# Attention with its eight PSUM banks split four and four and its outputs turned a step later; sums spread at the change of thirds

## The chip, the cores and the metric

One Trainium2 chip, of which the kernel uses one core. TensorE (PE) multiplies into PSUM, which this kernel uses as eight banks of 128 x 512 fp32; VectorE (DVE) and ScalarE (ACT) read PSUM, GpSimd (POOL) works on SBUF in this kernel, and SyncE (SP) issues the DMAs. The metric is the device time of one execution in microseconds.

## The reference, cut to what matters

```python
def phi(x):                                   # attention with random features
    proj = einsum('bhsd,md->bhsm', x, omega)
    h = proj - sum(x * x, -1) / 2
    return exp(h - max(h, -1)) / sqrt(m)
q_p, k_p = phi(q * scale), phi(k * scale)
kv = einsum('bhsm,bhsd->bhmd', k_p, v);  z = sum(k_p, 2)
attn = einsum('bhsm,bhmd->bhsd', q_p, kv) / (einsum('bhsm,bhm->bhs', q_p, z) + 1e-6)
x = attn as 2304 tokens x 512
x = (silu(x @ w_gate) * (x @ w_val)) @ w_out                 # 512 -> 1536 -> 512
P = sinkhorn(exp(x @ w_gate2), 8 rounds)                     # 2304 x 8
out = sum over 8 experts e of P[:, e] * (relu(x @ w1[e]) @ w2[e])   # 512 -> 1024 -> 512
```

Batch 4, 8 heads, 576 positions, head size 64, 128 features. All products are made of fp32r parts: a high part (a rounded copy) and a low part (the rest), three matmuls for each product.

## The kernel before

The whole program is issued by hand in one order (`manual_schedule`), so each engine runs what its instructions are in program order. The stages follow one another: attention, the first feed-forward (`moe1`), the first third of the tokens of the experts' layer (`moe2`), and the other two thirds (`thirds`).

**Attention** runs over 36 chunks of 128 x 512 (k tail, then k and q in turns: odd chunks are k, even ones q, up to a q tail at the end). A software pipeline (lines 651 to 666) does in step s for each entry (name, lag) of `ORDER` (line 63) the piece `name` of chunk s - lag. The pieces: `s0` squares x on GpSimd (three instructions, L478 to L481), `s0r` sums them on VectorE into ssq (L487), `s0n` scales that on GpSimd into nsq (L493); `s2p` makes 16 projections on TensorE into two banks (L515); `s2m` takes row maxima mx on VectorE (L519), `s2b` and `s2c` make hm (L523) and the bias bi (L527); `s2x` does eight exponentials on ScalarE out of the two banks (L534); `s3` transposes a q chunk (L559) or multiplies k with v (L555); `s3a` copies the result on ScalarE (L572, L568); `s4` makes numerators and denominators of a q chunk (L585); `s4d`, `s4r`, `s4n` divide on VectorE (L597, L602, L607); `s5` turns the quotient on TensorE (L617), `s5a` copies the high part on ScalarE (L628), and `s5b` takes the low part on VectorE (L633), both out of the bank that `s5` wrote. `pump` issues one piece of the conversion of the next stage's weights (lines 183 to 216), which spreads over ScalarE, VectorE and GpSimd.

`bank(use)` gives the next bank of the ring of that use; rings with the same banks share one turn. Of the eight banks tr3 takes two, and tr5, pr and nu share a ring of six. From step 37 on (line 652) `DRAIN` holds, and after each step `next(m1)` issues a unit of the next stage: 12 matmuls with 384 columns. x and the squares live in one tile of four parts: three for x, one for the squares.

**Thirds**: each step is a product pair over 14 slots: `quad_product` makes hidden units in seven products (a scheme of Strassen's kind) in three banks, each product a slot; `second_product` multiplies the hidden forms of the step before and adds them to sums. The hidden forms of a half are made by `a1` to `a4`, each put off by a slot by `after` (line 1385), as are the additions of sums and the stores at the change from the second to the last third (lines 1416 to 1430). `make_forms` splits the x forms of the next third, one a slot (lines 874 to 894).

Of the kernel before, what the change touches and what calls it, by code (L numbers as in the profile page):

```python
# [21 lines left out]
B, H, S, D = 4, 8, 576, 64  # L22
# [17 lines left out]
NG2 = 2 * E  # L40
# [10 lines left out]
class Kernel:  # L51
    def __init__(self, tc, x, v, vt, omega, wg, wv, wo, w2g, w1, w2, out):
# [7 lines left out]

    ORDER = [("s3a0", 3), ("s0r", 0), ("s5a", 7), ("s2p", 1), ("s2m0", 1), ("s40", 4), ("s41", 4),
# [3 lines left out]
    RINGS = dict(tr3=(0, 3), tr5=(4, 5, 6, 7, 2, 1), pr=(4, 5, 6, 7, 2, 1), nu=(4, 5, 6,  # L67
                 7, 2, 1), a=(0, 1, 2, 3), b=(4, 5, 6, 7))

    DRAIN = dict(RINGS, tr3=(4, 5), tr5=(4, 5), nu=(6, 7))  # L70


    EARLY = 1
# [325 lines left out]
    def attention(self, m1):  # L399
        tc, nc = self.tc, self.nc  # L400
        if True:
            af, ident = self.af, self.ident
            t0 = af.tile([P, 4, 512], F32, tag="t0", name="at0")
            t1 = af.tile([P, 2, 1024], F32, tag="t1", name="at1")
            t2 = af.tile([P, 4, 512], F32, tag="t2", name="at2")
            t3 = af.tile([P, 4, 512], F32, tag="t3", name="at3")
            t4 = af.tile([P, 5, 8, ZW], F32, tag="t4", name="at4")
# [6 lines left out]
            def turn(name, n):  # L414
                rot[name] = (rot.get(name, -1) + 1) % n
                return rot[name]
# [20 lines left out]
            NCH = len(chunks)  # L437
# [5 lines left out]
            def load(i):  # L443
                side, bp, hp, j = chunks[i]
                c = st[i]
                n = 8 if hp is None else 2 * hp + j
                k = turn("x", 3)
                xt = xts[turn("xt", 4)]
                c["xt"] = xt.rearrange("p (a t) -> p a t", t=P)
                c["x"] = t0[:, k].rearrange("p (a d) -> p a d", d=D)  # L450
                for w, t in ((1, xt), (0, t0[:, k])):
                    nc.sync.dma_start(t, self.x["qk".index(side), w, bp, n])
                c["idx"] = (lambda a, h: 2 * a + h) if hp is None else (lambda a, h: 4 * h + a)
# [15 lines left out]
            def s0(i):  # L469
                c = st[i]  # L470
                sqv = c["x"]
                if i < self.EARLY:
                    c["xx"] = t2[:, i].rearrange("p (a d) -> p a d", d=D)
                    c["ssq"] = sm.tile([P, 8], F32, tag="ssq", name=f"ssq{i}", bufs=4)
                    nc.scalar.activation(c["xx"], sqv, AF.Square)
                    return
                xx = t0[:, 3].rearrange("p (a d) -> p a d", d=D)
                nc.gpsimd.tensor_tensor(xx, sqv, sqv, op=ALU.mult)  # L478
                ssq = sm.tile([P, 8], F32, tag="ssq", name=f"ssq{i}", bufs=4)
                nc.gpsimd.tensor_tensor(xx[:, :, 0:32], xx[:, :, 0:32], xx[:, :, 32:64], op=ALU.add)  # L480
                nc.gpsimd.tensor_tensor(xx[:, :, 0:16], xx[:, :, 0:16], xx[:, :, 16:32], op=ALU.add)  # L481
                c["xx"], c["ssq"] = xx, ssq
# [153 lines left out]
            pump = lambda i: self.attn_pump()  # L636
# [11 lines left out]
            load(0)  # L648
            load(1)
            s0(0)  # L650
            for step in range(NCH + 7):
                if step == NCH + 1:
                    self.rings = self.DRAIN
                if step + 2 < NCH:
                    load(step + 2)
                if step == 0:
                    loadv(0)
                if step + 1 < NCH:
                    loadv(step + 1)
                for fn, n in order:  # L660
                    i = step - n
                    if 0 <= i < NCH:
                        fn(i)
                self.attn_hook(step)
                if step >= NCH + 1:
                    next(m1)

    def attn_hook(self, step):
# [205 lines left out]
    def make_forms(self):  # L874

        nc, v, g = self.nc, self.nc.vector, self.nc.gpsimd
        p0, p1, q0, q1 = self.quarters()
        x = self.spot
        low = None
        yield  # L880
        for n, src, eng in (("b11", x, g), ("t1", p0, v), ("t2", q1, v), ("t3", q0, v), (None, None, None), ("t4", p1, v),
                            ("b21", x, g), ("b22", p0, v), (None, None, None)):
            if low is not None:
                low()
                low = None
            if n == "t2":
                self.fetch_one(x, 0, 2)
            if n == "t3":
                self.fetch_one(p0, 1, 2)
            if n:  # L890
                h, l = [self.xslot(i, *self.XS[n]) for i in range(2)]
                nc.scalar.copy(h, src)
                low = lambda l=l, src=src, h=h, eng=eng: eng.tensor_tensor(l, src, f(h), op=ALU.subtract)
            yield
# [361 lines left out]
    def thirds(self, xs, t3, t4):  # L1256
        nc, af, v = self.nc, self.af, self.nc.vector
# [28 lines left out]
        def after(n, fn):  # L1286
            later.setdefault(now[0] + n, []).append(fn)
# [8 lines left out]
        def quad_product(step, j):  # L1296
            m = step % NG2
            k, i = divmod(j, 7)
            n = USE[i]
            c = live  # L1300
# [5 lines left out]
            g, first = {1: ("x", 1), 5: ("z", 1), 6: ("x", 0), 2: ("y", 1), 7: ("x", 0), 3: ("z", 0), 4: ("x", 0)}[n]  # L1306
            g = c[g]
# [7 lines left out]
            p0, p1 = [pb[m // 2 % 2][:, j * NBK:(j + 1) * NBK] for j in range(2)]  # L1315
            x, z, y = c["x"], c["z"], c["y"]
# [20 lines left out]
            if i == 0:  # L1337
                c["s"] = temp()
                nc.scalar.copy(c["s"], x)
            elif i == 1:  # L1340
                c["p"] = temp()
                nc.scalar.copy(c["p"], z)
            elif i == 2:
                c["u"] = temp()
                nc.scalar.copy(c["u"], x)  # L1345
            elif i == 3:
                v.tensor_tensor(c["s"], y, c["s"], op=ALU.add)
                gate(c["s"], c["s"], p0)
            elif i == 4:
                v.tensor_tensor(c["p"], x, c["p"], op=ALU.add)  # L1350
                gate(c["p"], c["p"], p1)
                hi(1, c["s"])
            elif i == 5:
                v.tensor_tensor(c["u"], z, c["u"], op=ALU.add)
                gate(c["u"], c["u"], p1)
                hi(3, c["p"])
                lo(1, c["s"], nc.gpsimd)
            else:
                r11, r22, r12, r21, t1, t2 = c["s"], c["p"], c["u"], temp(), temp(), temp()
                gate(r21, x, p0)  # L1360
                lo(3, r22, nc.gpsimd)

                def a1():
                    sub(t1, r12, r11)
                    sub(r12, r22, r12)
                    sub(t2, r22, t1)
                    hi(2, r21)
                    hi(5, t1)
                    lo(2, r21)

                def a2():
                    sub(r21, r21, t2)
                    hi(7, r12)
                    hi(6, t2)
                    lo(5, t1)
                    lo(7, r12)

                def a3():
                    hi(4, r21)
                    lo(6, t2)  # L1380

                def a4():
                    lo(4, r21)

                for d, fn in enumerate((a1, a2, a3, a4)):
                    after(d + 1, fn)

        def second_product(step, j):
            t, m = divmod(step, NG2)
# [26 lines left out]
            if m == NG2 - 1:  # L1416
                last = step > m
                sums = {1: [(2, 1)], 5: [(3, 5)], 6: [(1, 6), (3, 1)]}
                sums.setdefault(7 if last else 6, []).extend([(7, 1), (4, 7), (5, 7)])
                for k, (d, c) in enumerate(sums.get(n, ())):  # L1420
                    def add(d=d, c=c, eng=nc.gpsimd if d == 5 else v):
                        eng.tensor_tensor(a[d], a[d], a[c], op=ALU.add)

                    if last:
                        add()
                    else:
                        after(k + 1, add)
                for d in {2: (2,), 7: (5,) if last else (), 6: (3,) if last else (3, 5, 4)}.get(n, ()):
                    c, i = {2: (0, 0), 4: (2, 0), 3: (0, 1), 5: (2, 1)}[d]
                    after(0 if last else {2: 3, 3: 5, 5: 8, 4: 7}[d], lambda c=c, i=i, d=d: self.store_block(t + 1, c, i, a[d]))  # L1430

        sums = xg = iter(())
        for g in range(self.STEPS):
# [107 lines left out]
```

## Time and profile before

| | |
|---|---|
| time, median of 3 runs (lowest to highest) | 2070.68 us (2070.24 to 2072.59) |
| the profiled execution: time | 2070.69 us |
| the profiled execution: span of its instructions | 2068.9 us |
| mean granted clock of TensorE | 0.996 |
| TensorE busy | 2017.9 us (98%) |
| VectorE, ScalarE, GpSimd busy | 1369.6, 806.5, 1044.0 us (66%, 39%, 50%) |

Read it so: TensorE is busy almost throughout, so what it does not do matters most; the 40 slices of the page show it below nine tenths only in the first slices, which are attention. Busy time of TensorE is time in which some matmul is in flight, not its peak rate.

### The profile page before, as it was taken

How to read it: one execution, taken by the hardware profiler on the slowest of the kernel's cores; microseconds unless marked ns; L12 is line 12 of the kernel's file. 1: busy time of each engine (PE TensorE's matmuls, PEld its weight loads, DVE VectorE, ACT ScalarE, POOL GpSimd, SP SyncE). 2: the span in 40 equal slices, each digit the busy share in tenths (PEclk: the TensorE clock that was granted, in tenths of full speed). 3: DMA queues.
4: the chain of work that ended last, by engine and by line, in shares of the span. 5: the costliest groups of instructions: out<-in, count | busy, mean ns of one | idle time of the engine just before them, and what ended most of it. 6: DMA issues, size and time to landing. Idle time of an engine off the chain costs nothing.

```text
span 2068.9 us, 34032 instructions
## 1 busy us (share of the span) xinstructions
PE 2017.9 (98%) x12556; PEld 1948.7 (94%) x12556; DVE 1369.6 (66%) x2283; ACT 806.5 (39%) x1805; POOL 1044.0 (50%) x1054
## 2 busy tenths in 40 slices
PE   6889999999999999999999999999999999999998
PEld 6679999999998899899898999999999999999998
DVE  6877788778657644444445666666678666666666
ACT  6784433333335443343342423233333433332322
POOL 6865666656515454554752443434464534343443
PEclk9999999999999999999999999999999999999999
DMA  7644556546236567677678788888878888888784
GB/s 236 198 145 128 178 164 188 183 149 204 82 113 239 198 236 260 220 270 261 221 267 289 251 264 257 261 261 282 276 248 276 273 260 262 258 265 256 245 271 152
DMA packets 238134, 467.85 MB, mean 226 GB/s; under 512 B 20272, under 2 KB 110096, under 8 KB 233872
## 3 DMA queue, kind: packets, MB, share of 16 engines
q1 hardware_dynamic: 237968, 465.68, 68.3%
q8 instruction: 99, 1.62, 0.3%
q14 instruction: 67, 0.55, 0.1%
HBM read 340.25 MB, written 125.35 MB: 225 GB/s over the span
## 4 chain that ended last, share of the span: by engine, by line
PE 90%; DVE 5%; POOL 3%; issue 1%; ACT 1%; DMA 1%; SPq 0%; DVEq 0%; POOLq 0%; ACTq 0%
PE bank L1064 12%; PE bank L1312 7%; PE bank L1314 7%; PE bank L1313 7%; PE pair L1403 7%; PE pair L1405 7%; PE pair L1404 7%; PE bank L704 5%; PE bank L706 5%; PE bank L705 5%; PE bank L1005 4%; PE bank L1007 4%; PE bank L1006 4%; PE bank L736 2%; PE bank L738 2%; PE bank L737 2%
## 5 line engine op out<-in xcount | busy, mean ns | idle before, releaser
L1415 DVE TENSOR_TENSOR sums<-pair,sums 128x768 f32<-128x768 f32 x209 | 198.6, 951 | 43.6 <-PE pair L1405 43.6
L1312 PE MATMUL bank<-xh,ar 128*128 128x384 f32 x564 | 188.7, 335 | 2.4 <-ACT mt L1345 2.0
L1313 PE MATMUL bank<-xl,ar 128*128 128x384 f32 x564 | 188.4, 334 | 0.0
L1314 PE MATMUL bank<-xh,ar 128*128 128x384 f32 x564 | 188.4, 334 | 0.0
L1080 DVE SCALAR_TENSOR_TENSOR ac<-bank,mt,ac 128x512 f32<-128x512 f32 x84 | 63.1, 751 | 131.3 <-PE bank L1064 131.3
L1403 PE MATMUL pair<-xh,ar 128*128 128x384 f32 x344 | 115.0, 334 | 0.1
L1405 PE MATMUL pair<-xh,ar 128*128 128x384 f32 x344 | 114.9, 334 | 0.0
L1404 PE MATMUL pair<-xl,ar 128*128 128x384 f32 x344 | 114.9, 334 | 0.0
L1312 PEld LDWEIGHTS bank<-xh,ar 128*128 128x128 f32 x564 | 105.8, 188 | 3.4 <-ACT mt L1345 2.7
L1313 PEld LDWEIGHTS bank<-xl,ar 128*128 128x128 f32 x564 | 105.9, 188 | 0.0
L1314 PEld LDWEIGHTS bank<-xh,ar 128*128 128x128 f32 x564 | 105.9, 188 | 0.0
L718 ACT CAST ar<-mt 128x384 fp32r<-128x384 f32 x72 | 37.0, 514 | 169.4 <-DVE mt L715 169.4
L704 PE MATMUL bank<-xh,ar 128*128 128x384 f32 x288 | 96.7, 336 | 0.1
L706 PE MATMUL bank<-xh,ar 128*128 128x384 f32 x288 | 96.2, 334 | 0.0
L706 PE MATMUL bank<-xh,ar1b 128*128 128x384 f32 x288 | 96.2, 334 | 0.0
L705 PE MATMUL bank<-xl,ar 128*128 128x384 f32 x288 | 96.2, 334 | 0.0
L704 PE MATMUL bank<-xh,ar1b 128*128 128x384 f32 x288 | 96.2, 334 | 0.0
L705 PE MATMUL bank<-xl,ar1b 128*128 128x384 f32 x288 | 96.2, 334 | 0.0
L534 ACT ACTIVATE at<-bank,bi 128x128 f32<-128x128 f32 x288 | 78.4, 383 | 36.7 <-DVE bi L527 23.7
L1005 PE MATMUL bank<-xh,ar 128*128 128x384 f32 x264 | 89.1, 338 | 0.9 <-DVE mt L1039 0.6
L1007 PE MATMUL bank<-xh,ar 128*128 128x384 f32 x264 | 88.6, 335 | 0.1
L1006 PE MATMUL bank<-xl,ar 128*128 128x384 f32 x264 | 88.4, 335 | 0.0
(369 smaller groups left out, 6652.4 us busy)
## 6 DMA issues: line engine op xcount, KB each, us to landing
ar<-w2forms SPq DMA_DIRECT2D x144, 512.0 KB, 4.4
ar<-w1forms SPq DMA_DIRECT2D x141, 512.0 KB, 4.8
ar1b<-w1forms SPq DMA_DIRECT2D x62, 512.0 KB, 4.8
ar1b<-w2forms SPq DMA_DIRECT2D x61, 512.0 KB, 4.4
w2forms<-ar SPq DMA_DIRECT2D x224, 128.0 KB, 4.0
w1forms<-ar SPq DMA_DIRECT2D x22, 1280.0 KB, 6.9
sumsraw<-in_w_dram SPq DMA_DIRECT2D x32, 512.0 KB, 4.5
w2forms<-sumsraw SPq DMA_DIRECT2D x128, 128.0 KB, 2.7
```

The lines of the kernel that those rows point to most:

```text
L704: nc.tensor.matmul(t, hi[:, c, fs], self.xh[:, c, cs], start=(c == 0), stop=False)
L705: nc.tensor.matmul(t, hi[:, c, fs], self.xl[:, c, cs], start=False, stop=False)
L706: nc.tensor.matmul(t, lo[:, c, fs], self.xh[:, c, cs], start=False, stop=(c == KC - 1))
L1005: nc.tensor.matmul(g, ah[:, c, :], bh[:, c, :], start=(first and c == 0), stop=False, skip_group_check=not first)
L1064: nc.tensor.matmul(y, a, w[:, fi % 2, ds], start=(first and x == 0 and k == 0 and fi == fis[0]), stop=(last and x == 1 and fi == fis[-1]))
L1312: nc.tensor.matmul(g, w[:, 0, d], bh[:, d, :], start=bool(first and d == 0), stop=False, skip_group_check=not first)
L1313: nc.tensor.matmul(g, w[:, 0, d], bl[:, d, :], start=False, stop=False, skip_group_check=not first)
L1314: nc.tensor.matmul(g, w[:, 1, d], bh[:, d, :], start=False, stop=(d == 1), skip_group_check=not first)
L1403: nc.tensor.matmul(y, w[:, k, 0, ds], h, start=(k == 0), stop=False)
L1404: nc.tensor.matmul(y, w[:, k, 0, ds], l, start=False, stop=False)
L1405: nc.tensor.matmul(y, w[:, k, 1, ds], h, start=False, stop=(k == 1))
L1415: v.tensor_tensor(a[n], pair, a[n], op=ALU.add)
```

## The change

It changes five things. (1) In attention the projections (pr) have banks 4 to 7 for themselves, and tr3, tr5 and nu share a ring of banks 0 to 3; in the drain all three use banks 4 to 7. (2) The outputs are turned with lag 7 instead of 6, their high and low parts are made with lag 8 instead of 7, and the low part s5b comes second in the order, ahead of the maxima; s0r moves behind s2c, and s5 ahead of s3. The loop has one step more, and the first unit of the next stage comes a step later, so that their number stays. (3) x has two parts of its tile, the squares two. (4) In `thirds` the pieces a1 to a4 of the very first half, and of the last half before the change of thirds, are put off by two slots each instead of one; the additions and stores at the change from the second third to the last come later. (5) `make_forms` splits t4 last instead of fifth, with an empty slot more.

```diff
--- before.py
+++ after.py
@@ -60,14 +60,15 @@
 
 
 
-    ORDER = [("s3a0", 3), ("s0r", 0), ("s5a", 7), ("s2p", 1), ("s2m0", 1), ("s40", 4), ("s41", 4),
-             ("s2m1", 1), ("s2b", 1), ("s2c", 1), ("s3a1", 3), ("s0", -1), ("pump", 2), ("s2", 0),
-             ("s30", 2), ("s2x0", 1), ("s31", 2), ("s4d0", 4), ("s0n", 0), ("s5", 6), ("s5b",
-             7), ("s2x1", 1), ("s4d1", 4), ("pump", 3), ("s4r", 4), ("s4n0", 4), ("s4n1", 4)]
-    RINGS = dict(tr3=(0, 3), tr5=(4, 5, 6, 7, 2, 1), pr=(4, 5, 6, 7, 2, 1), nu=(4, 5, 6,
-                 7, 2, 1), a=(0, 1, 2, 3), b=(4, 5, 6, 7))
-
-    DRAIN = dict(RINGS, tr3=(4, 5), tr5=(4, 5), nu=(6, 7))
+    ORDER = [("s3a0", 3), ("s5a", 8), ("s5b", 8), ("s2p", 1), ("s2m0", 1), ("s40", 4), ("s41", 4),
+             ("s2m1", 1), ("s2b", 1), ("s2c", 1), ("s0r", 0), ("s3a1", 3), ("s0", -1), ("pump", 2), ("s2", 0),
+             ("s5", 7), ("s30", 2), ("s2x0", 1), ("s31", 2), ("s4d0", 4), ("s0n", 0),
+             ("s2x1", 1), ("s4d1", 4), ("pump", 3), ("s4r", 4), ("s4n0", 4), ("s4n1", 4)]
+    RINGS = dict(tr3=(0, 3, 2, 1), tr5=(0, 3, 2, 1), pr=(4, 5, 6, 7), nu=(0, 3, 2, 1),
+                 a=(0, 1, 2, 3), b=(4, 5, 6, 7))
+
+    DRAIN = dict(RINGS, tr3=(4, 5, 6, 7), tr5=(4, 5, 6, 7), nu=(4, 5, 6, 7))
+
 
 
     EARLY = 1
@@ -444,7 +445,7 @@
                 side, bp, hp, j = chunks[i]
                 c = st[i]
                 n = 8 if hp is None else 2 * hp + j
-                k = turn("x", 3)
+                k = turn("x", 2)
                 xt = xts[turn("xt", 4)]
                 c["xt"] = xt.rearrange("p (a t) -> p a t", t=P)
                 c["x"] = t0[:, k].rearrange("p (a d) -> p a d", d=D)
@@ -474,7 +475,7 @@
                     c["ssq"] = sm.tile([P, 8], F32, tag="ssq", name=f"ssq{i}", bufs=4)
                     nc.scalar.activation(c["xx"], sqv, AF.Square)
                     return
-                xx = t0[:, 3].rearrange("p (a d) -> p a d", d=D)
+                xx = t0[:, 2 + turn("xx", 2)].rearrange("p (a d) -> p a d", d=D)
                 nc.gpsimd.tensor_tensor(xx, sqv, sqv, op=ALU.mult)
                 ssq = sm.tile([P, 8], F32, tag="ssq", name=f"ssq{i}", bufs=4)
                 nc.gpsimd.tensor_tensor(xx[:, :, 0:32], xx[:, :, 0:32], xx[:, :, 32:64], op=ALU.add)
@@ -648,7 +649,7 @@
             load(0)
             load(1)
             s0(0)
-            for step in range(NCH + 7):
+            for step in range(NCH + 8):
                 if step == NCH + 1:
                     self.rings = self.DRAIN
                 if step + 2 < NCH:
@@ -662,7 +663,7 @@
                     if 0 <= i < NCH:
                         fn(i)
                 self.attn_hook(step)
-                if step >= NCH + 1:
+                if step >= NCH + 2:
                     next(m1)
 
     def attn_hook(self, step):
@@ -878,8 +879,9 @@
         x = self.spot
         low = None
         yield
-        for n, src, eng in (("b11", x, g), ("t1", p0, v), ("t2", q1, v), ("t3", q0, v), (None, None, None), ("t4", p1, v),
-                            ("b21", x, g), ("b22", p0, v), (None, None, None)):
+        wait = (None, None, None)
+        for n, src, eng in (("b11", x, g), ("t1", p0, v), ("t2", q1, v), ("t3", q0, v), wait, ("b21", x, g), wait,
+                            ("b22", p0, v), wait, ("t4", p1, v), wait):
             if low is not None:
                 low()
                 low = None
@@ -1382,8 +1384,9 @@
                 def a4():
                     lo(4, r21)
 
+                gap = 2 if (step, k) in ((0, 0), (NG2 - 1, 1)) else 1
                 for d, fn in enumerate((a1, a2, a3, a4)):
-                    after(d + 1, fn)
+                    after(gap * d + 1, fn)
 
         def second_product(step, j):
             t, m = divmod(step, NG2)
@@ -1417,17 +1420,17 @@
                 last = step > m
                 sums = {1: [(2, 1)], 5: [(3, 5)], 6: [(1, 6), (3, 1)]}
                 sums.setdefault(7 if last else 6, []).extend([(7, 1), (4, 7), (5, 7)])
-                for k, (d, c) in enumerate(sums.get(n, ())):
+                for d, c in sums.get(n, ()):
                     def add(d=d, c=c, eng=nc.gpsimd if d == 5 else v):
                         eng.tensor_tensor(a[d], a[d], a[c], op=ALU.add)
 
                     if last:
                         add()
                     else:
-                        after(k + 1, add)
+                        after({(1, 6): 1, (7, 1): 2, (3, 1): 7, (5, 7): 8, (4, 7): 9}.get((d, c), 1), add)
                 for d in {2: (2,), 7: (5,) if last else (), 6: (3,) if last else (3, 5, 4)}.get(n, ()):
                     c, i = {2: (0, 0), 4: (2, 0), 3: (0, 1), 5: (2, 1)}[d]
-                    after(0 if last else {2: 3, 3: 5, 5: 8, 4: 7}[d], lambda c=c, i=i, d=d: self.store_block(t + 1, c, i, a[d]))
+                    after(0 if last else {2: 3, 3: 9, 5: 11, 4: 11}[d], lambda c=c, i=i, d=d: self.store_block(t + 1, c, i, a[d]))
 
         sums = xg = iter(())
         for g in range(self.STEPS):
```

## Rows read from the trace of the kernel before

**Rows 1.** Windows: span; busy (instructions) of PE, PEld, DVE, ACT, POOL; clock; DMA share, GB/s
```profile
38.67:145.50 106.83, 87.25 (x1469) 76.16 (x1468) 89.32 (x233) 82.39 (x269) 84.44 (x120) 0.98 0.61 190
...
200.00:550.00 350.00, 350.00 (x2021) 350.00 (x2020) 273.93 (x411) 125.41 (x247) 212.25 (x204) 1.00 0.56 172
1100.00:1150.00 50.00, 47.50 (x248) 43.67 (x247) 33.98 (x47) 20.23 (x38) 19.13 (x16) 1.00 0.82 275
1550.00:1650.00 100.00, 96.04 (x549) 94.58 (x548) 75.78 (x106) 40.26 (x79) 47.41 (x40) 1.00 0.82 276
```

**Rows 2.** Waits of TensorE, 0 to 165: who waited for whom, total, times, longest
```profile
PE bank L515 <- ACT at L534: 15.0, 14, 1.4
```

**Rows 3.** Groups, 38.67 to 145.50: shapes, count, busy, mean ns; idle before, and releasers
```profile
L519 DVE TENSOR_REDUCE mx<-bank 128x4 f32<-128x512 f32 x53 | 34.0, 682 | 7.9 <-ACT at L534 7.3 <-PE bank L515 0.7
...
L523 DVE SCALAR_TENSOR_TENSOR hm<-mx,nsq 128x8 f32<-128x8 f32 x26 | 10.0, 384 | 5.1 <-POOL nsq L493 2.7
...
L527 DVE SCALAR_TENSOR_TENSOR bi<-hm,nsq 128x8 f32<-128x8 f32 x26 | 9.1, 350 | 0.9
...
L487 DVE TENSOR_REDUCE ssq<-at 128x8 f32<-128x128 f32 x26 | 7.3, 279 | 3.4 <-POOL at L481 3.4
...
L204 DVE SCALAR_TENSOR_TENSOR cv<-m1raw,cv 128x512 int32<-128x512 int32 x5 | 4.5, 896 | 0.0
...
L197 DVE TENSOR_SCALAR cv<-m1raw 128x512 int32<-128x512 int32 x4 | 1.7, 413 | 0.0
```

**Rows 4.** Timeline of VectorE, 137.5 to 150: start, duration; idle before and releaser
```profile
137.68 1.29 DVE L519 TENSOR_REDUCE mx<-bank 128x4 f32<-128x512 f32 x2 [0.74 <-ACT at L534]
...
142.27 0.66 DVE L523 SCALAR_TENSOR_TENSOR hm<-mx,nsq 128x8 f32<-128x8 f32 x1
142.96 0.17 DVE L527 SCALAR_TENSOR_TENSOR bi<-hm,nsq 128x8 f32<-128x8 f32 x1
...
143.54 0.76 DVE L607 TENSOR_TENSOR at<-bank,rec 128x256 f32<-128x256 f32 x2
144.21 0.28 DVE L487 TENSOR_REDUCE ssq<-at 128x8 f32<-128x128 f32 x1
145.50 1.29 DVE L519 TENSOR_REDUCE mx<-bank 128x4 f32<-128x512 f32 x2 [1.01 <-ACT at L534]
...
147.09 0.17 DVE L527 SCALAR_TENSOR_TENSOR bi<-hm,nsq 128x8 f32<-128x8 f32 x1
...
148.04 1.29 DVE L519 TENSOR_REDUCE mx<-bank 128x4 f32<-128x512 f32 x2 [0.18 <-PE bank L515]
```

**Rows 5.** Timelines of ScalarE and, last row, VectorE, 147 to 155
```profile
147.37 2.18 ACT L534 ACTIVATE at<-bank,bi 128x128 f32<-128x128 f32 x8 [0.50 <-DVE bi L527]
149.39 0.33 ACT L568 ACTIVATE at<-bank 128x132 f32<-128x132 f32 x1
...
152.40 0.66 ACT L628 CAST xh<-bank 128x512 fp32r<-128x512 f32 x1
...
153.09 0.69 DVE L633 TENSOR_TENSOR xl<-bank,xh 128x512 fp32r<-128x512 f32 x1 [2.12 <-ACT xh L628]
```

**Rows 6.** Timeline of GpSimd, beside rows 4
```profile
142.17 0.73 POOL L480 TENSOR_TENSOR at<-at 128x256 f32<-128x256 f32 x1
```

**Rows 7.** Windows of 4 us in attention, columns as in rows 1
```profile
52.00:56.00 4.00, 2.57 (x32) 2.09 (x32) 3.01 (x9) 2.98 (x11) 3.68 (x6) 0.91 0.21 74
56.00:60.00 4.00, 4.00 (x74) 3.75 (x72) 2.85 (x8) 3.58 (x12) 3.59 (x6) 0.66 0.71 181
```

**Rows 8.** Timelines of TensorE and VectorE in the thirds
```profile
1134.13 0.45 PE L1312 MATMUL bank<-xh,ar 128*128 128x384 f32 x1 [1.68 <-ACT mt L1345]
...
1582.85 0.45 PE L1403 MATMUL pair<-ar1b 128*128 128x384 f32 x1 [1.93 <-DVE sums L1415]
...
1607.43 0.44 PE L1312 MATMUL bank<-xh,ar2b 128*128 128x384 f32 x1 [1.28 <-DVE mt L1350]
...
1578.82 3.11 DVE L1332 TENSOR_TENSOR xl<-mt,xh 128x384 fp32r<-128x384 f32 x3
...
1605.96 0.95 DVE L1422 TENSOR_TENSOR sums<-sums,sums 128x768 f32<-128x768 f32 x1
```

## Prediction

> **What bounds the kernel now.** I read the stages first [rows 1]. From 200 to 1100 us, and again through the thirds, TensorE is busy nearly without a gap, so nothing that this change does to another engine can shorten those stretches. It has gaps in three places that the change touches: attention, where from 38.67 to 145.50 us it is busy 87.25 of 106.83 us; the first step of the thirds (2.50 us idle between 1100 and 1150); the change from the second to the third third (3.96 us idle between 1550 and 1650). Attention is followed by work that keeps TensorE full, so a microsecond there is one at the end.
>
> Next, who holds attention. VectorE, ScalarE and GpSimd are each busy about 80% of [rows 1]; none is full, so it is a loop of waits. I count it on VectorE, by the start of the row maxima (mx, L519): the one at 38.67 us belongs to step 9, the one at 145.50 to step 35, so 26 steps, or 13 pairs, took 106.83 us, 8.22 us a pair. The last pair, without weight conversions, took 7.82 (137.68 to 145.50) [rows 4]. I call a step whose projections (s2p) are of a q chunk a Q-step (odd step) and the others K-steps. VectorE's time not spent at work is in [rows 3]: mx waited 7.9 us, nearly all for ScalarE, whose exponentials hold the second bank of the next projections (TensorE lost 15.0 us to that over all of attention, [rows 2]); ssq waited 3.4 for GpSimd; hm waited 2.7 for nsq. Beyond that hm and bi, which take 0.17 alone, average 0.384 and 0.350: 26 x 0.21 + 26 x 0.18 = 10.2 us. In [rows 6] with [rows 4] one sees why: hm started at 142.27, a GpSimd instruction ran to 142.90, and hm ended just behind it. Sum: 24.2 us, so VectorE's work proper is about 82.6.
>
> **The change part by part: banks and second square buffer.** Projections get four banks of their own, used again two steps later, when their exponentials are long read; the others get four. The bank waits go (7.9). With two buffers for the squares GpSimd no longer waits for ssq of the same step, and ssq moves behind bi: the waits of 3.4 and 2.7 go. The price is that x has two buffers, not three: SP may issue a load two steps ahead only when GpSimd has read the old one. GpSimd comes back to that buffer two steps, some 8 us, later; I take that as cover for the load, and put it at nothing (were it late, GpSimd and then nsq would be). Behind the waiting load SP holds the v load and the next turned x, which are used a step or more later. The transposes of s5 stand in a Q-step ahead of the s3 products, which wait for exponentials anyway: nothing.
>
> **The outputs.** This is where I see the loss. s5a and s5b move from lag 7 to lag 8, that is from Q-steps to K-steps, and s5b now stands first on VectorE, ahead of the maxima. s5b needs s5a. s5a is first on ScalarE in that step, but behind all eight exponentials of the Q-step before, and these need bi of that Q-step, VectorE's last instruction but ssq. So VectorE ends bi, does ssq, and stands until ScalarE has done eight exponentials and a copy; queued behind the waiting s5b are mx, hm, bi of the K-step, and for that bi wait the next exponentials. Before, s5b stood behind bi and its s5a ahead of the exponentials: no wait.
>
> The new loop, from rows without conversions. Q-step bi start to exponentials' start: 147.09 to 147.37, 0.28 [rows 4, 5]. Eight exponentials until the next ScalarE instruction starts: 2.02 [rows 5]. s5a and start of s5b: 152.40 to 153.09, 0.69; s5b itself 0.69 [rows 5]. mx start to bi start: 145.50 to 147.09, 1.59 [rows 4]. That is 5.27 for the half that begins with the Q-step's bi. The other half: K-step bi to s4n 0.58, s4n to ssq 0.67, ssq 0.28 [rows 4], mx to bi 1.59: 3.12. Sum 8.39 a pair. Instructions on VectorE start a little before the one ahead has ended, so between 8.2 and 8.4; I take 8.3. This is a floor: 13 x 8.3 = 107.9.
>
> On top of it: the conversions' VectorE instructions, 24 in the window, 4.5 us for the five of L204 down to 1.7 for the four of L197 [rows 3], 12.7 in all. Those in Q-steps disappear in the new wait; those in K-steps lie on the loop: half of 12.7, less what starts early, 5 (4 to 7). ScalarE's conversions that fall between exponentials and s5a: +1.2 (0 to 2, a few copies of about 0.66, [rows 5]). Collisions with GpSimd: 10.2 now, fewer when GpSimd stands still around the K-step's hm; +2.5 (0 to 5). Window: 107.9 + 5 + 1.2 + 2.5 = 116.6, against 106.83: **+9.8** (+3.8 to +16).
>
> Ends of attention. The last mx comes 2.54 after the one before it (145.50 to 148.04); then it stands in a step with an s5b: 1.59 + 0.28 + 2.02 + 0.69 + 0.69 = 5.27, say **+2.6**. In the drain the second product of s4 at step 38 gets the bank of the outputs turned at step 37, which s5a and s5b of step 38 read, behind three more copies on ScalarE: some 2.7 us from the last exponentials; TensorE's first unit of the next stage, today right behind the last transposes, now stands behind that product: **+1.7** (0 to 3). The number of such units, and of conversions, stays. Steps 1 to 8 turn no outputs yet, and only gain GpSimd's freedom: (3.4 + 2.7) / 26 = 0.23 a step, **-1.9** (0 to -3). Attention: +12.2.
>
> **The thirds.** In the first step the split of the low forms is issued every second slot. Today TensorE waits 1.68 us at 1134.13 for a ScalarE copy (L1345) [rows 8] queued behind casts that wait for GpSimd; with the casts a slot later that copy runs when its product is done. VectorE then is late at the next use of the bank by a part of it: -1.3. At the change of thirds TensorE waits 1.93 at 1582.85 for the accumulation L1415, which stood behind three low parts (3.11 us); two of them are now issued behind it: -1.9. It waits 1.28 at 1607.43 for L1350, behind an addition of sums L1422 (0.95); that addition is one of those put off, -0.9, and a small wait after it, -0.3. The additions put off come in the next step, where the accumulation is a ScalarE copy, so VectorE has room: nothing. The order in which the new x forms are split moves t4 to last; it is used last, so nothing. Together **-4.5**. Bounds: 0, and all of TensorE's idle time there, -6.5.
>
> Sum, against the profiled execution's own 2070.69 (span 2068.9, 1.8 around it; the median of three is 2070.68, the same): 2070.7 + 12.2 - 4.5 = **2078.4 us**.
>
> **The rivals.** (a) *The banks were it.* If VectorE's new wait falls where it would have waited anyway, only the gains count: -(7.9 + 3.4 + 2.7) = -14.0, -4.5 from the thirds: 2052; half of it, 2061. For it: 15.0 us of bank waits are real. Against: the order on ScalarE and VectorE is the program's in all rows that I read, and nothing else holds mx that long. The Trainium skill (Perfetto Trace Analysis, section Optimization Strategy) says that gaps repeating on an engine can mean too little PSUM for the next tile; by that rule this rival would come true; the rows show such a gap, but on a loop that has a second closing edge.
> (b) *A draw.* The loop at its floor of 8.2, conversions at 4, no collisions, no cost in the drain: 3.8 + 2.6 - 3 = +3.4, with -4.5: 2069.6. Decided by how much of the conversions falls on K-steps.
> (c) *TensorE's clock.* With a longer pair TensorE stands more. Around 52 to 60 us it fell once: busy 2.57 of 4 us at a granted clock of 0.91, then 0.66 in the next 4 us [rows 7], a mix of 2.4 and 1.2 GHz. If it fell in every second pair, for 2 us of products done at half speed, 1 us each: 6 or 7 us more, 2085. The Trainium skill (TensorE: Matmul & The Clock Gate, section on cycling through PSUM banks) tells of a kernel whose clock swings because TensorE idles briefly between groups. Against: the other pairs of rows 1's window average 0.98.
> (d) *The thirds do nothing*, because VectorE's backlog only moves: 2083.
>
> **How the numbers follow.** Forecast and (d): 0.59. (b): 0.22. (a): 0.13. (c): 0.06. What a measurement of this kernel can tell from no change is about 0.2%, 4.1 us: below 2066.5 or above 2074.8. (a) is faster, most of (b) the same with a little on either side: faster 0.14, same 0.22, slower 0.64. The forecast's own bounds give 2070 to 2090 (attention +3.4 to +20, thirds -2 to -5); reaching into (b) and the near half of (a): 2064 to 2088.
>
> **What would show it.** VectorE's L633 with an idle time before it of some 2.5 us, released by ScalarE's L628, in every pair; mx without waits for L534's banks, ssq without waits for GpSimd; pairs of 8.5 to 9.3 us; the last mx near 159 us. In the thirds no wait at L1345 in the first step and none near 1.9 us at L1403. Wrong if L633 follows without idle time, or if the pair is under 8.2.

## The result: slower, by twice what was forecast, and the profile after

The changed kernel takes 2086.98 us (2085.21 to 2088.32), against 2070.48 for the kernel before beside it: a ratio of 1.0081, interval 1.0069 to 1.0092. The profiled execution took 2085.21 (span 2083.0), 14.1 us more span than before; this is what is accounted for below.

The same windows as [rows 1], now on the changed kernel; its ninth to thirty-fifth maxima lie from 36.35 to 159.94 us, and the stages up to the thirds start some 18 us later. Columns as in [rows 1].

```profile
36.35:159.94 123.59, 87.15 (x1470) 75.02 (x1470) 88.28 (x234) 81.20 (x267) 85.58 (x119) 0.94 0.54 166
200.00:560.00 360.00, 360.00 (x2079) 360.00 (x2078) 281.41 (x416) 130.13 (x256) 225.40 (x215) 1.00 0.57 177
1115.00:1165.00 50.00, 48.72 (x257) 45.09 (x256) 32.61 (x46) 21.02 (x40) 18.00 (x14) 1.00 0.83 283
1565.00:1665.00 100.00, 98.91 (x567) 97.78 (x566) 80.31 (x110) 41.59 (x83) 50.35 (x42) 1.00 0.84 281
```

All engines do the work that they did in attention, in 123.59 us instead of 106.83. In the window around the first step of the thirds TensorE is idle 1.28 us (2.50 before), around the change of thirds 1.09 (3.96 before). VectorE's groups in the attention window, which answer to [rows 3]; lines of the changed kernel are one higher there:

```profile
L520 DVE TENSOR_REDUCE mx<-bank 128x4 f32<-128x512 f32 x53 | 33.9, 680 | 0.0
L524 DVE SCALAR_TENSOR_TENSOR hm<-mx,nsq 128x8 f32<-128x8 f32 x26 | 10.8, 414 | 2.7
...
L634 DVE TENSOR_TENSOR xl<-bank,xh 128x512 fp32r<-128x512 f32 x13 | 9.0, 692 | 30.9 <-ACT xh L629 30.9
L528 DVE SCALAR_TENSOR_TENSOR bi<-hm,nsq 128x8 f32<-128x8 f32 x26 | 8.8, 340 | 0.9
L488 DVE TENSOR_REDUCE ssq<-at 128x8 f32<-128x128 f32 x26 | 7.2, 277 | 0.0
```

Every old wait is gone: mx had 7.9 us, ssq 3.4, hm 2.7 for GpSimd. One new wait of 30.9 us took their place: the low part (s5b, L634) for the high part (s5a, L629), 13 times, 2.4 us each on average. The last pair has no conversions and shows it bare; first VectorE, then ScalarE (start, duration, instruction, idle before):

```profile
151.58 1.28 DVE L520 TENSOR_REDUCE mx<-bank 128x4 f32<-128x512 f32 x2
...
153.34 0.17 DVE L528 SCALAR_TENSOR_TENSOR bi<-hm,nsq 128x8 f32<-128x8 f32 x1
153.42 0.28 DVE L488 TENSOR_REDUCE ssq<-at 128x8 f32<-128x128 f32 x1
156.30 0.69 DVE L634 TENSOR_TENSOR xl<-bank,xh 128x512 fp32r<-128x512 f32 x1 [2.60 <-ACT xh L629]
156.91 1.28 DVE L520 TENSOR_REDUCE mx<-bank 128x4 f32<-128x512 f32 x2
```

```profile
153.62 2.17 ACT L535 ACTIVATE at<-bank,bi 128x128 f32<-128x128 f32 x8
155.63 0.64 ACT L629 CAST xh<-bank 128x512 fp32r<-128x512 f32 x1
```

VectorE ends bi, does ssq and stands 2.60 us, until ScalarE has done eight exponentials and the copy; only then come the next maxima. The next pair begins at 159.94: 8.36 us. The waits of TensorE that remain in the thirds, which answer to [rows 8]:

```profile
1154.06 0.45 PE L1314 MATMUL bank<-xh,ar 128*128 128x384 f32 x1 [0.87 <-DVE last L1352]
...
1598.33 0.45 PE L1406 MATMUL pair<-ar1b 128*128 128x384 f32 x1 [0.21 <-DVE sums L1418]
...
1622.09 0.44 PE L1314 MATMUL bank<-xh,ar2b 128*128 128x384 f32 x1 [0.47 <-DVE mt L1352]
```

The wait of 1.68 for ScalarE in the first step is gone; the next use of the bank waits 0.87 for VectorE (0.40 before, at 1136.89). At the change of thirds 1.93 fell to 0.21 and 1.28 to 0.47.

The account by places: the ninth maxima come 2.3 us earlier (36.35, 38.67), the window is 16.8 longer, the last interval of maxima 2.6 longer (5.15, 2.54), the way from the last maxima to the next stage's first output product 1.5 longer (22.5, 21.06). That is 18.5 us at that product (187.6, 169.1), carried on to the first product of the thirds (1120.8 to 1139.5, 18.7). Within the thirds 4.6 come back.

### The profile page after: what moved, and what is told of

It is laid out like the page before. It is cut to its first block, busy times and chain, and to the rows that moved or that the text cites. A ratio compares the mean times of both kernels' runs of the same rounds, so it can differ in the third digit from the quotient of the medians.

```text
span 2083.0 us, 33931 instructions
## 1 busy us (share of the span) xinstructions
PE 2019.1 (97%) x12556; PEld 1948.3 (94%) x12556; DVE 1370.7 (66%) x2283; ACT 804.8 (39%) x1805; POOL 1046.1 (50%) x1054
## 4 chain that ended last, share of the span: by engine, by line
PE 89%; DVE 6%; ACT 3%; issue 1%; POOL 0%; DMA 0%; SPq 0%; DVEq 0%; ACTq 0%
PE bank L1066 12%; PE bank L1316 7%; PE bank L1314 7%; PE bank L1315 7%; PE pair L1406 7%; PE pair L1408 7%; PE pair L1407 7%; PE bank L707 5%; PE bank L705 5%; PE bank L706 5%; PE bank L1007 4%; PE bank L1009 4%; PE bank L1008 4%; PE bank L737 2%; PE bank L739 2%; PE bank L738 2%
```

## The experiments

The table has the stretch from the ninth to the thirty-fifth maxima, the start of the next stage's first output product, and the time; each is told below. The first two columns are read from the profiled execution, the time is the median of several. The last three kernels ran once each; in them the conversions were moved or cut, so their times are not comparable.

| kernel | stretch, us | next stage, us | time, us |
|---|---|---|---|
| before | 106.83 | 169.1 | 2070.7 |
| after | 123.59 | 187.6 | 2086.98 |
| e2, outputs alone | 121.01 | 186.2 | 2087.89 |
| e4, banks and buffers alone | 107.29 | 168.0 | 2073.07 |
| e1, low part behind the sums | 115.31 | 177.9 | 2074.50 |
| e3, thirds alone | 106.51 | 167.7 | 2064.97 |
| f5, e3 and second squares | 106.15 | 167.6 | 2064.29 |
| g1, high part ahead of the exponentials | 97.65 | 161.8 | 2058.81 |
| h1, g1 with old banks and buffers | 116.51 | 179.7 | 2077.04 |
| h2, h1 with second squares | 102.21 | 162.8 | 2058.85 |
| f1, after, conversions late | 108.62 | | |
| f3, after, no GpSimd conversions | 114.35 | | |
| f2, before, conversions late | 92.42 | | |

**The parts alone.** e3 is the kernel before with the new code of the thirds.

> The kernel before with the part in the thirds alone (pieces two slots apart, additions and stores later, t4 split last). Theory: 4.5 us less, 2066.0 (2065 to 2067). Rival (VectorE's backlog only moves, the waits come later): 2070 to 2071.

Measured 2064.97, ratio 0.9974 (0.9963 to 0.9984), just under the stated 2065; span 2062.9, 6.0 less than before. Of this -1.4 was there before the thirds began to differ (167.7 against 169.1, with the same code up to there, so it is scatter between executions) and -4.6 lies within the thirds. The part gives what was forecast, and alone it beats both kernels. e2 is the kernel before with the outputs alone:

```
-  ... ("s0r", 0), ("s5a", 7), ("s2p", 1) ... ("s5", 6), ("s5b", 7), ("s2x1", 1)
+  ... ("s0r", 0), ("s5a", 8), ("s5b", 8), ("s2p", 1) ... ("s5", 7), ("s2x1", 1)
-  for step in range(NCH + 7):
+  for step in range(NCH + 8):
```

> The kernel before with one part of the change alone: outputs turned with lag 7, parts made with lag 8, s5b ahead of the maxima, one step more; banks, x buffers and thirds as before. Theory: the same idle time of some 2.6 us before s5b in each pair, a pair from 8.2 to 9.0 to 10.0 us, the time from 2070.5 to 2080 to 2095. Rival one (ring of four): no change in attention, 2068 to 2074.

Measured 2087.89, ratio 1.0083 (1.0068 to 1.0098). (In its drain, at step 37, `s5` takes a bank whose transposes have not yet been copied, so some values come out wrong; this lies behind the stretch that is read.) Two of VectorE's groups, 37.29 to 158.30:

```profile
L518 DVE TENSOR_REDUCE mx<-bank 128x4 f32<-128x512 f32 x53 | 33.9, 680 | 0.0
...
L632 DVE TENSOR_TENSOR xl<-bank,xh 128x512 fp32r<-128x512 f32 x13 | 9.0, 691 | 25.4 <-ACT xh L627 25.4
```

With the old banks the same new wait appears, and the maxima wait for no bank: the bank waits go because VectorE is late, not because there are more banks. By spans, e2 with the thirds' gain would be at 2085.9 - 4.6 = 2081.3, and the changed kernel is at 2083.0: banks and buffers, with the moves of s0r and s5, earned nothing beside the late low part. e4 is the kernel before with the banks and buffers alone.

> The kernel before with the banks four and four and two buffers each for x and the squares, outputs and thirds as before. Theory: the projections' wait for a bank and ssq's wait for GpSimd go and nothing comes in their place, 7 to 14 us less: 2057 to 2064. Rival one (ring of four is the loss): TensorE waits for the ring instead, 2075 to 2090. Rival three (x with two buffers is late): GpSimd waits for the x load and the time is above 2072.

Measured 2073.07, ratio 1.0009 (1.0000 to 1.0019): no gain. The first theory is missed; the time is the one stated for rival three. But e4 doesn't measure the banks by themselves. With the outputs turned at lag 6, in the K-step, five turns of a ring of four fall in that step, and the fifth puts the transposes of s5 into the bank that holds the first numerators before they are scaled. So one half of the outputs of 15 of the 18 q chunks comes out wrong, and TensorE waits for that bank. From its waits, 36 to 146 (who waited for whom, total, times, longest):

```profile
PE bank L618 <- DVE den L598: 11.2, 8, 2.5
...
POOL at L479 <- DMA at<-in_x_dram: 8.1, 6, 2.0
```

The second row is a late load of x, which the prediction put at nothing; here it is real. That two buffers of x make it is not shown: f5 below has three, and there GpSimd waits 6.1 us for such loads in its stretch, while in the changed kernel, with two, it waits for none. e4 shows one thing more: the ring of four needs the outputs a step later.

**The place of the low part.** e1 is the changed kernel with s5b behind the sums:

```
-  ("s3a0", 3), ("s5a", 8), ("s5b", 8), ("s2p", 1) ... ("s0r", 0), ("s3a1", 3)
+  ("s3a0", 3), ("s5a", 8), ("s2p", 1) ... ("s0r", 0), ("s5b", 8), ("s3a1", 3)
```

> The changed kernel with one line moved: s5b stands behind s0r instead of ahead of the maxima. Theory (VectorE stands at s5b for eight exponentials and a copy, 2.6 us a pair): the idle time before s5b falls to under 1 us, a pair from 9.5 us to 7.6 to 8.2, the time from 2087 to 2055 to 2066. Rival one (the ring of four banks is too small: the transposes of s3 wait for the bank that s5b reads, 27.6 us in the changed kernel): s5b reads later, so those waits stay or grow and the time stays at 2083 to 2092. Rival two (TensorE's clock falls four times in attention instead of once): the clock falls as often and the time stays within 4 us of 2087.

Measured 2074.50, ratio 1.0016 (1.0007 to 1.0026), between the expectations. (In its drain, at step 38, numerators take the bank of an output before its low part is made, so one chunk's low part comes out wrong; this too lies behind the stretch.) From its waits, 37.74 to 153.05:

```profile
PE bank L560 <- DVE xl L634: 24.9, 13, 2.7
...
DVE mx L520 <- PE bank L516: 19.8, 17, 2.7
```

The low part now waits 0.2 us in all, and the stretch is 8.3 us shorter. But the ring of four has a second edge: the first s3 transposes of the K-step take the bank of the outputs, and stand on TensorE until s5b has read it; the next projections stand behind them. So with this ring the low part can't go late either. What is left is to let the high part be early. g1 is the changed kernel with s5a in the step of the transposes, ahead of its exponentials:

```
-  ("s3a0", 3), ("s5a", 8), ("s5b", 8), ("s2p", 1) ... ("s5", 7), ("s30", 2), ("s2x0", 1)
+  ("s3a0", 3), ("s5b", 8), ("s2p", 1) ... ("s5", 7), ("s30", 2), ("s5a", 7), ("s2x0", 1)
```

> The kernel after with one move: ScalarE's copy of the high part stands in the step in which the outputs are turned, ahead of that step's exponentials, instead of at the head of the next step; the low part stays first on VectorE. Theory (the price of the change is the low part that waits on VectorE for a high part queued behind eight exponentials): the low part's idle time of 31 us in the stretch from the ninth to the thirty-fifth maxima falls below 6, the stretch from 123.6 to between 97 (VectorE's own busy time there) and 108, and the time to 2062 to 2073. Rival (the ring of four banks, or GpSimd's collisions, takes the place of that wait): 2080 to 2088.

Measured 2058.81, ratio 0.9942 (0.9926 to 0.9959): 28 us below the changed kernel by one copy's place, and below the stated 2062; the stretch is within what was stated. VectorE's groups, 39.05 to 136.70:

```profile
L520 DVE TENSOR_REDUCE mx<-bank 128x4 f32<-128x512 f32 x53 | 34.0, 681 | 0.8 <-PE bank L516 0.8
L524 DVE SCALAR_TENSOR_TENSOR hm<-mx,nsq 128x8 f32<-128x8 f32 x26 | 12.3, 475 | 2.7
L528 DVE SCALAR_TENSOR_TENSOR bi<-hm,nsq 128x8 f32<-128x8 f32 x26 | 10.8, 415 | 0.9
...
L634 DVE TENSOR_TENSOR xl<-bank,xh 128x512 fp32r<-128x512 f32 x13 | 8.9, 681 | 0.3
```

VectorE stands nowhere for longer than the short gaps between its instructions: it is now the bound. The theory stands.

**Banks or squares.** h1 is g1 with the rings and buffers of before (three x, one buffer of squares; in the drain the changed kernel's rings), h2 is h1 with a second buffer of squares in free room:

```
-  xx = t0[:, 3].rearrange("p (a d) -> p a d", d=D)
+  xx = (t0[:, 3], bx[:, 4608:5120])[turn("xx", 2)].rearrange("p (a d) -> p a d", d=D)
```

> The order of the work as in the last variant (outputs a step later, high part ahead of that step's exponentials, low part first on VectorE, new change of thirds), but with the banks and buffers of before: a ring of six and one of two, three buffers of loads and one of squares. Theory (the banks are of little weight once the low part has no wait): 2058 to 2061. Rival (the new banks are what lets VectorE run without a gap): the maxima wait again for banks, some 7 us in the stretch from the ninth to the thirty-fifth, and the sums for GpSimd, some 3 us; 2064 to 2070.

> The last variant (order with the high part ahead of the exponentials, banks of before, three buffers of loads) with a second buffer of squares in free room elsewhere, so that against the variant of 2058.8 only the banks differ. Theory (the waits of 30 us of hm for GpSimd's nsq come from the one buffer of squares, and the banks are of little weight): those waits fall below 3 us, the stretch from the ninth to the thirty-fifth maxima to 97 to 101 us, the time to 2058 to 2062. Rival (the ring of six brings the maxima's bank waits back): 7 us or more of waits of the maxima for a bank, 2064 to 2068.

h1: 2077.04, ratio 1.0028 (1.0017 to 1.0039), outside both expectations. Two of VectorE's groups in its stretch, 37.98 to 154.49:

```profile
L519 DVE TENSOR_REDUCE mx<-bank 128x4 f32<-128x512 f32 x53 | 33.9, 681 | 1.5 <-PE bank L515 1.5
...
L523 DVE SCALAR_TENSOR_TENSOR hm<-mx,nsq 128x8 f32<-128x8 f32 x26 | 4.4, 168 | 29.7 <-POOL nsq L493 28.4
```

The maxima hardly wait for banks, but hm waits 28.4 us for GpSimd: in this order ssq stands behind bi, and with one buffer GpSimd can't begin the next squares before that ssq. h2, where this alone is mended, takes 2058.85, ratio 0.9943 (0.9926 to 0.9960), as g1 does to 0.04 us. Its stretch, 102.21 us, is over what was expected and 4.6 over g1's, with 5.7 us of waits of the maxima for projections; but g1's ninth maxima come 3.55 us later (39.05, 35.50), and the last ones stand 0.9 apart (139.78, 140.71). The section on the hardware shows where TensorE's clock fell in each of the two, at different places. So the four banks, with two buffers of x for three, are worth nothing that these runs can tell (2058.14 to 2059.53 with them, 2057.47 to 2060.42 without), and the second buffer of squares 18 us in this order. In the old order it is worth next to nothing; f5 is e3 with the same edit:

> The kernel before with the new change of thirds and with a second buffer for the squares in free room elsewhere, so that the loads keep three buffers. Forecast's step (the sums' waits for GpSimd, some 3.4 us of idle time, are on the path): 2061 to 2063.5. Rival (the sums are not on the path, since the next maxima wait for the exponentials all the same): 2064.3 to 2065.7, as with the thirds alone (2064.97).

Measured 2064.29 (2063.51 to 2065.25), ratio 0.9970 (0.9958 to 0.9981): the rival's value, 0.7 below e3. ssq no longer waits for GpSimd (3.4 in e3), nor hm for nsq (2.7), but the stretch is only 0.4 us shorter. The rival's reason is a small part of it: the maxima wait 8.3 us (7.0 in e3). Most went elsewhere: VectorE's conversions take 18.9 us in the stretch instead of 13.0. One of their five groups, first e3, then f5:

```profile
L206 DVE TENSOR_SCALAR m1raw<-cv 128x512 int32<-128x512 int32 x5 | 2.0, 410 | 0.0
```

```profile
L206 DVE TENSOR_SCALAR m1raw<-cv 128x512 int32<-128x512 int32 x5 | 4.2, 843 | 0.0
```

That GpSimd, now free to run ahead, holds these up as it does hm and bi is likely, but not shown.

**The conversions.** f1 and f2 are the kernels after and before with no conversion issued in attention, f3 is the kernel after without GpSimd's share there:

```
 def attn_pump(self):                      # f1, f2
-    self.pump(1)
+    pass
 self.attn_hook(step)
+if step == NCH:
+    self.flush()

+if not self.bare:                         # f3, at the three GpSimd instructions
     nc.gpsimd.tensor_tensor(...)
```

> The kernel after, but no conversion of expert weights is issued within the attention: all six waiting tasks run between the attention and the first layer, so the whole time is longer and is not what is read. Read is the stretch from the ninth to the thirty-fifth pair of maxima (123.6 us in the kernel after). Theory (the conversions, GpSimd's above all, were priced too low in the forecast): the stretch falls to 13 x 8.36 = 109 us (107 to 112), the single hm and bi cost 0.17 to 0.2 us each, and the low part still waits 2.2 to 2.6 us for the high part in every pair. Rival (the pairs are long for another cause, TensorE's clock or the turn of the banks): the stretch stays above 118.

> The kernel after, but within the attention GpSimd's three operations of every conversion are left out (the expert weights converted there have no low part and keep only the upper bits), while VectorE's and ScalarE's operations of the same conversions stay; GpSimd zeroes the low parts once at the start instead. Theory (small VectorE operations are held up behind GpSimd's conversions): hm falls from a mean of 0.41 and bi from 0.34 to at most 0.22, and the stretch from the ninth to the thirty-fifth pair of maxima from 123.6 to 111 to 115 us. Rival (VectorE's and ScalarE's own share of the conversions makes the length, or GpSimd's squares hold hm and bi up): the stretch stays at 119 or more; hm stays above 0.35 if it is the squares.

> The kernel before, but no conversion of expert weights is issued within the attention; all six waiting tasks run between the attention and the first layer, so the whole time is longer and is not what is read. Read is the stretch from the ninth to the thirty-fifth pair of maxima: 106.83 us with the conversions. Theory one (the conversions cost the old order about what they cost the new one, 123.6 - 108.6 = 15.0 us, since they stand on VectorE in both): the stretch falls to 91 to 95 us. Theory two (the old order hid them behind its waits for banks, and the new order exposes them, which is the part of the loss that the forecast lacks): it falls only to 98 to 104 us, and the waits of the maxima for banks grow beyond 6.9 us.

f1 falls to 108.62 us, f3 to 114.35, f2 to 92.42; in each the first theory's number. hm does not quite fall as stated: 0.245 in f1 (0.17 to 0.2 was stated) and 0.226 in f3 (at most 0.22). VectorE's groups in these stretches, first f1, then f3 (lines three higher), then f2:

```profile
L634 DVE TENSOR_TENSOR xl<-bank,xh 128x512 fp32r<-128x512 f32 x13 | 9.0, 692 | 33.9 <-ACT xh L629 33.9
...
L524 DVE SCALAR_TENSOR_TENSOR hm<-mx,nsq 128x8 f32<-128x8 f32 x26 | 6.4, 245 | 2.7
L528 DVE SCALAR_TENSOR_TENSOR bi<-hm,nsq 128x8 f32<-128x8 f32 x26 | 4.3, 167 | 0.9
```

```profile
L637 DVE TENSOR_TENSOR xl<-bank,xh 128x512 fp32r<-128x512 f32 x13 | 9.0, 692 | 31.0 <-ACT xh L632 31.0
...
L527 DVE SCALAR_TENSOR_TENSOR hm<-mx,nsq 128x8 f32<-128x8 f32 x26 | 5.9, 226 | 2.7
L531 DVE SCALAR_TENSOR_TENSOR bi<-hm,nsq 128x8 f32<-128x8 f32 x26 | 4.3, 167 | 0.9
```

```profile
L519 DVE TENSOR_REDUCE mx<-bank 128x4 f32<-128x512 f32 x53 | 34.2, 686 | 13.6 <-ACT at L534 12.7 <-PE bank L515 0.9
L523 DVE SCALAR_TENSOR_TENSOR hm<-mx,nsq 128x8 f32<-128x8 f32 x26 | 10.2, 392 | 2.7
```

From f1 to the kernel after is 15.0 us, the conversions' whole price in the new order: 9.2 of it GpSimd's (123.59 - 114.35), 5.7 VectorE's and ScalarE's (114.35 - 108.62). In f3 hm and bi are 9.4 us shorter in sum than in the kernel after (19.6 to 10.2), which is GpSimd's share by the second way. In the old order the conversions cost 14.4 (106.83 - 92.42), although the maxima's waits for ScalarE grow without them, from 7.3 to 12.7.

## Why the prediction was right in kind and short in size

**Banks and squares: the waits went, and were worth nothing.** All three waits named are gone, and rival (a) falls: in e2 the bank waits go without any new bank, and in f5 the squares' buffer earns 0.7 us in the old order. What the four banks alone would earn in the old order is not shown, since e4 mixes them with a ring that is too small. The Trainium skill's Perfetto Trace Analysis, section Optimization Strategy, says that a gap that repeats can mean too little PSUM for the next tile. By it rival (a) would have come true; the measurement decides against it here: g1 and h2 differ in their banks and buffers of x, and take the same time.

**Outputs: the mechanism is as told.** L634 waits in each pair, released by L629, 2.6 us without conversions (f1: 33.9 in 13) and 2.4 with them (30.9), where some 2.5 was named; the pair without conversions takes 8.36 us (f1: 12 of 13 pairs within 8.20 to 8.38, the other 8.47), where 8.3 was taken and 8.39 was the sum: 0.7 us short over 13 pairs.

**Collisions with GpSimd: the term that was too small.** It was put at 2.5 (0 to 5), on the ground that GpSimd would stand still around the hm of the K-step; f3 measures 9.2. The changed kernel's timelines, GpSimd and VectorE, show why:

```profile
94.73 0.46 POOL L482 TENSOR_TENSOR at<-at 128x128 f32<-128x128 f32 x1
95.15 1.26 POOL L182 TENSOR_TENSOR ar<-cv,ar 128x512 fp32r<-128x512 f32 x1
```

```profile
95.16 1.28 DVE L524 SCALAR_TENSOR_TENSOR hm<-mx,nsq 128x8 f32<-128x8 f32 x1
96.47 0.97 DVE L528 SCALAR_TENSOR_TENSOR bi<-hm,nsq 128x8 f32<-128x8 f32 x1
```

This is a Q-step, where VectorE doesn't wait. There GpSimd's order of squares and then conversion starts from the ssq just ahead, and its squares end about when VectorE comes to hm: here L182 starts 0.01 us before hm. hm takes 1.28 us instead of 0.17, until L182 ends. hm or bi is held to 0.95 us or more in Q-steps 11, 17, 21, 27 and 31, but only in K-steps 16 and 26; in the other 11 of 13 K-steps hm takes 0.17. So the ground given held for the K-steps, and the Q-steps were left out. The Trainium skill (SBUF — State Buffer, section Who interferes with whom) has the rule: a VectorE operation with two inputs in SBUF is held for the whole of a GpSimd operation that reads SBUF and began first. The trace agrees, 95.16 + 1.28 against 95.15 + 1.26.

The terms for VectorE's and ScalarE's own conversions, 5 + 1.2, were right: 5.7. So the stretch came to 108.6 + 5.7 + 9.2 = 123.6, where 107.9 + 6.2 + 2.5 = 116.6 was forecast: 6.7 of the 7.0 missing are collisions. Rival (b), which put them at nothing, falls with this.

Why it went wrong: I counted the collisions as falling because VectorE waits more. They are of two kinds, and only one fell. What hm and bi take beyond 52 times 0.17 is 10.3 us before and 10.8 after. Without conversions it is 5.8 in the old order (f2) and 1.9 in the new one (f1): that is GpSimd's squares, and it fell. The rest, some 4.5 before and 8.9 after by these differences (9.4 after by f3), is GpSimd's conversions, and it grew. f2 shows too that the old order paid 14.4 for its conversions in all, so the forecast 8.7 for the new one would have been a gain of 5.7 that nothing in the profile gave. By f1 and f2 the order itself costs 16.2 (108.62 - 92.42), and the conversions 0.6 more.

**Ends.** Last interval +2.6 as forecast, drain +1.5 against +1.7. Early steps -2.3 against -1.9, but not for the reason given: the first maxima already start 2.92 us earlier (9.25 to 6.33), since ssq no longer stands ahead of them, and the steps from there to the ninth take 0.6 longer (29.42 to 30.02).

**Thirds.** -4.5 forecast (its own terms add up to -4.4), -4.6 measured in the changed kernel and in e3. By the idle time of [rows 1]'s two windows -1.2 in the first step (-1.3 forecast) and -2.9 at the change (-3.1). Rival (d) falls.

**Clock.** In the stretch the granted clock was below 0.86 in four places instead of one, each some 8 us; the first, in windows of 4 us:

```profile
52.00:56.00 4.00, 2.71 (x25) 2.25 (x25) 3.25 (x11) 1.67 (x7) 2.62 (x5) 0.85 0.43 95
56.00:60.00 4.00, 4.00 (x62) 3.48 (x62) 2.50 (x7) 4.00 (x14) 3.18 (x6) 0.72 0.90 278
```

It isn't seen in the pairs: conversions repeat every five pairs, and the pair at 36.35, where the windows from 36 to 48 us have 1.00, took 9.73 us, that at 84.06, with 0.81 in its first 4 us, 9.71. Rival (c) is not the cause.

The sum was 12.2 - 4.5 = +7.7; it is 18.7 - 4.6 = +14.1 by the profiled spans. The time is at the upper end of the range because the window, at +16.8, passed the upper bound of +16 given for it; the other terms came close to their middle values, and the time lies in the range by that. For the same reason two of the signs failed: the pairs take 8.36 to 10.11 us, 9.5 on average, where 8.5 to 9.3 was named, and the last maxima start at 165.09, not near 159. That the medians differ by 2 us more than the profiled executions is not explained by any row.

## What to carry to other kernels

An instruction put first on an in-order engine is only as early as its producer: look where the producer stands in its own queue, and move the two together. A wait that disappears from a profile is a gain only if nothing was due behind it; undoing the parts one by one showed here that the banks earned nothing that could be told, the buffer of squares earned 18 us in one order and under 1 in the other, and one copy's place decided over 28 us. Work of an engine that shares something with the bound must be priced by where it falls, not by its average.

## What was not expected of the hardware

TensorE's clock cost nothing that could be seen in the changed kernel, but it did in h2, where VectorE waits for TensorE: its pairs at 43.09 and 120.56 took 9.78 and 10.23 us, its others 6.91 to 7.85, 7.47 on average. Windows of 4 us in h2, columns as in [rows 1]:

```profile
48.00:52.00 4.00, 3.94 (x45) 3.57 (x46) 2.68 (x10) 3.66 (x15) 3.68 (x6) 0.60 0.16 60
52.00:56.00 4.00, 3.92 (x78) 3.37 (x76) 2.88 (x8) 3.15 (x10) 2.65 (x5) 1.00 0.77 233
126.00:130.00 4.00, 3.65 (x38) 3.06 (x36) 2.13 (x9) 3.67 (x13) 3.68 (x6) 0.57 0.26 60
```

Not all of these 2.3 and 2.8 us is the clock. The pair at 82.50 stands at the same point of the conversions' turn of five pairs, the clock was full there, and it took 7.85 us. In it VectorE waited 0.84 us for TensorE, and in the two slow pairs 1.98 and 2.46: 1.1 and 1.6 more. The waits of the maxima, in the first slow pair and in the one at 82.50:

```profile
52.87 1.29 DVE L519 TENSOR_REDUCE mx<-bank 128x4 f32<-128x512 f32 x2 [1.32 <-PE bank L515]
...
90.35 1.29 DVE L519 TENSOR_REDUCE mx<-bank 128x4 f32<-128x512 f32 x2 [0.84 <-PE bank L515]
```

g1 had the same ahead of its ninth maxima; the eighth, second fence (VectorE's timeline), waited 2.11 us for TensorE:

```profile
28.00:32.00 4.00, 3.51 (x36) 2.93 (x36) 3.72 (x11) 2.15 (x9) 3.68 (x6) 0.55 0.68 217
```

```profile
35.49 0.69 DVE L520 TENSOR_REDUCE mx<-bank 128x4 f32<-128x512 f32 x1 [2.11 <-PE bank L516]
```

The same 32 products of s4, in h2 at a clock of 0.60 (near the lower level, 1.2 of 2.4 GHz), and in g1 where the clock was full; TensorE had stood 2.22 us for ScalarE before the first:

```profile
48.06 2.18 PE L585 MATMUL bank<-at,at 128*64 128x66 f32 x32 [2.22 <-ACT at L534]
```

```profile
95.25 1.16 PE L586 MATMUL bank<-at,at 128*64 128x66 f32 x32
```

And in g1 the collisions grow rather than shrink: hm and bi take 23.1 us, 14.3 more than 52 times 0.17, against 19.1 and 10.3 in the kernel before. With VectorE full, that is the largest thing left in this stage that is not work.
